# The second attention's values: split float32r products, or float32 products with two experts in one array

## The chip, the cores and the metric

One of the eight cores of a Trainium2 chip runs the whole program; there is one launch. The metric is the device time of that launch in microseconds (us), as a median over runs. Lower is better. TensorE is the matrix engine (PE in the profile, PEld for its weight loads), VectorE is DVE, ScalarE is ACT, GpSimd is POOL, and SyncE (SP) issues most of the DMA transfers.

## What is computed

Three layers follow each other: a linear attention, a feed-forward layer with a layer norm, and a mixture of four attention experts (here "the second attention"). Only the last is touched. Cut from the reference, with B = 8 batches, S = 576 positions, D = 512, E = 4 experts, head size 64:

```python
for e in range(E):
    q = x @ wq[e]
    k = x @ wk[e]
    v = x @ wv[e]
    scores = scale * (q @ k.transpose(0, 2, 1))
    causal = np.triu(np.ones((S, S), dtype=bool), 1)
    scores = np.where(causal, -1000000000.0, scores)
    scores = scores - scores.max(-1, keepdims=True)
    a = np.exp(scores)
    a /= a.sum(-1, keepdims=True) + 1e-09
    ye = a @ v @ wo[e]
    for kk in range(K):
        mask = topk[:, :, kk] == e
        out += mask[..., None] * w[:, :, kk:kk + 1] * ye
```

The change is in how `a @ v` is formed and in when.

## The kernel before, in words

**Numbers in two halves.** Nearly every product of the kernel keeps float32 accuracy by a split: an operand is written as a float32r value plus a float32r rest (ACT writes the first, DVE subtracts it from the source and writes the second; the helper `split`, L180 and L181), and three or four float32r products are added up in PSUM. All products go through the helper `mm`, so they carry line L174 in the profile and are told apart by their output tile: `psh` and `acc` or `psc` for the feed-forward layer, `psqk` for queries and keys, `psv` for values, `pssc` for scores, `pst` for transposes, `py` for attention times values, `pso` for the output projection.

**Where products are float32.** A few early products take float32 operands as they are: `pkv` in the first attention (two heads, each 64 columns of the array, one into PSUM partitions 0 to 63, the other into 64 to 127; 112 or 128 rows, 66 moving columns, called one head after the other for five chunks) and `po<-qT,kvw` (128 columns, 288 moving columns). A float32 product shows as two matmul records.

**The last part of the program** (from about 820 us) goes batch by batch. While the attention of one batch (`back`) runs, the feed-forward layer of the next (`mlp2`) and its projections (`qk_proj`, `v_proj`) run beside it: `weave` deals the pieces of the two lists alternately, and the framework's scheduler then sets the order of the instructions on each engine. For the last batch (`order[-1]`) little is left to deal between.

**A unit** is one row block (128 queries; the fifth block has 64 and takes both experts in one unit, `PairUnit`) of one pair of experts r (r = 0, 1; within it j = 0, 1 are the two experts). It makes scores (`pssc`, then one DVE instruction that adds the mask and finds the bound, L1369), the exponentials (ACT, L1377), the scale by sum and gate (POOL, L1389), and in `turn` transposes the weights on PE (`pst`, L1401 and L1450). `put` copies them out of PSUM as two float32r tiles: ACT writes `aTh` (L1420), then DVE writes the rest `aTl` (L1421), which needs `aTh`.

**values.** Rows are taken in groups (`GROUPS`: blocks 0 and 1, then 2 to 4; in the last batch's r = 1 `LASTG`: 0, then 3 and 4, then 1 and 2). Before, all groups of r = 0 come first and then those of r = 1. When the units of a group are done, `values` forms for each expert j the sum over key blocks kb. The tile `vv` holds for each expert 128 columns: 64 of v's float32r value and 64 of its rest. The stationary operand is these 128 columns, the moving one is `aTh`, then `aTl`: two products for a key block (the last key block has 64 keys, and its rows carry both halves in one product). PSUM `py` then has the two parts in its two halves; ACT copies the lower half out (`ytmp`, L1472), DVE adds the two (`yf`, L1473), and with both experts done `split` writes `yh` and `yl`, which `proj` multiplies with wo.

```python
th, tl = aT[j]
...
parts = (th,) if kb == NQ - 1 else (th, tl)
for t in parts:
    mm(py[:, c0:gn], vt, t[:, offs[kb]:offs[kb] + n], kb == 0 and t is th,
       kb == grp[-1] and t is parts[-1])
tmp = atp.tile([D, GW], F32, tag="ytmp", name="ytmp")
nc.scalar.activation(tmp[:, :gn], py[D:2 * D, :gn], AF.Copy)
nc.vector.tensor_tensor(yf[j * D:(j + 1) * D, :gn], py[:D, :gn], tmp[:, :gn], op=ALU.add)
```

For the group of blocks 0 and 1 the moving columns are 256 and 128 for the two key blocks; for blocks 2 to 4 they are 320, 320, 320, 192 and 64.

Of the kernel before, what the change touches and what calls it, by code (L numbers as in the profile page):

```python
# [18 lines left out]
P = 128  # L19
# [110 lines left out]
def tile_kernel(ctx: ExitStack, tc: tile.TileContext, q, k, v, g_ln, w1, w2, w_gate, wq, wk, wv, wo, out):  # L130
# [1135 lines left out]
    def v_proj(x2s, res):  # L1266
        def one(c):
            if c == 0:
                res["v"] = qkp.tile([P, NQ, E, 2, D], F32R, tag="vv", name="vv")
                res["lg"] = qkp.tile([P, NQ, E], F32, tag="lg", name="lg", bufs=2)  # L1270
                nc.gpsimd.memset(res["lg"], 0.0)
            vv, lg, wvg = res["v"], res["lg"], moe["vg"]
            n = min(P, S - c * P)
            ps = psm("psv")
            h, o = divmod(c * P, T)
            if o + n <= T:
                x = x2s[h][:, :, :, o:o + n]
            else:
                x = res["xj"]
            for cc in range(NDC):  # L1280
                mm(ps[:n, :VG], x[:, 0, cc, :], wvg[:, 0, cc, :], cc == 0, False)
                mm(ps[:n, :VG], x[:, 0, cc, :], wvg[:, 1, cc, :], False, False)
                mm(ps[:n, :VG], x[:, 1, cc, :], wvg[:, 0, cc, :], False, cc == NDC - 1)
            pv = ps[:n, :E * D].rearrange("p (e d) -> p e d", e=E)

            for t in [vv[i:i + n, c] for i in range(0, P, n)]:
                nc.scalar.activation(t[:, :, 0, :], pv, AF.Copy)
                nc.vector.tensor_tensor(t[:, :, 1, :], pv, raw(t[:, :, 0, :]), op=ALU.subtract)
            nc.vector.tensor_copy(lg[:n, c, :], ps[:n, E * D:VG])  # L1289
            for g0, g1 in GCUTS:  # L1290
                if c == g1 - 1:
                    gates(g0, g1)
# [44 lines left out]
            o += gn - max(0, kb * P - g0)  # L1337
        return g0, gn, offs, o

    GW, AW = (max(layout(g)[i] for g in GROUPS + LASTG) for i in (1, 3))  # L1340

    class Unit:

# [8 lines left out]
        def scores(self, j):  # L1352
            r, i, m, w = self.r, self.i, self.m, self.w
            if j == 0:
                self.st = atp.tile([P, 2, 4], F32, tag="st", name="st", bufs=4)
            sm = self.sm[j] = atp.tile([P, S], F32, tag="sm", name="sm", bufs=4)
            mo = NM - i * P
            q = self.res[r, "q"][:, j, i * P:i * P + m]
            self.part(sm, m, 0, w, [(j, q)], mask[:m, mo:mo + w], j, 0)
            self.last = 0  # L1360
# [31 lines left out]
        def turn(self, j):  # L1392

            i, m, sm = self.i, self.m, self.sm[j]
            g0, _, offs, _ = layout(self.grp)
            if i == self.grp[0]:
                self.aT[j] = tuple(atp.tile([P, AW], F32R, tag=nm, name=nm, bufs=2) for nm in ("aTh", "aTl"))
            pt = ps_t.tile([P, 512], F32, tag="t", name="pst")
            for kb in range(i + 1):
                kw = min(P, S - kb * P)  # L1400
                nc.tensor.transpose(pt[:kw, kb * m:kb * m + m], sm[:m, kb * P:kb * P + kw], ident[:m, :m])  # L1401
            dst = [offs[kb] + i * P - max(g0, kb * P) for kb in range(i + 1)]
            self.put(j, pt[:, :(i + 1) * m].rearrange("p (n m) -> p n m", m=m), P, dst, m)

        def put(self, j, src, kw, dsts, m):

            kb = 0
            while kb < len(dsts):

                n = 1  # L1410
                while kb + n < len(dsts) and dsts[kb + n] - dsts[kb + n - 1] == dsts[kb + 1] - dsts[kb]:
                    n += 1
                step = dsts[kb + 1] - dsts[kb] if n > 1 else m
                th, tl = (t[:, dsts[kb]:dsts[kb] + m] for t in self.aT[j])
                oh, ol = (bass.AP(tensor=o.tensor, offset=o.offset, ap=[list(o.ap[0]), [step, n], [1, m]])
                          for o in (th[:kw], tl[:kw] if kw == P else th[kw:]))
                from_ = src[:, kb:kb + n]
                if n == 1:
                    oh, ol, from_ = oh[:, 0], ol[:, 0], src[:, kb]
                nc.scalar.activation(oh, from_, AF.Copy)  # L1420
                nc.vector.tensor_tensor(ol, from_, raw(oh), op=ALU.subtract)  # L1421
                kb += n

    class PairUnit(Unit):
# [6 lines left out]
        def scores(self, j):  # L1431
            if j == 0:
                self.st = atp.tile([P, 2, 4], F32, tag="st", name="st", bufs=4)
                self.sm[0] = atp.tile([P, S], F32, tag="sm", name="sm", bufs=4)
            c0 = j * T
            qs = [(e, q_pads[self.r][:, e, :]) for e in range(2)]
            self.part(self.sm[0], P, c0, c0 + T, qs, tail_mask if j else mask[:, :T], 0, j)
            self.last = 1
# [4 lines left out]
        def turn(self, j):  # L1443
            i, sm = self.i, self.sm[0]
            g0, _, offs, _ = layout(self.grp)
            pt = ps_t.tile([P, 512], F32, tag="t", name="pst")
            blocks = range(i) if j == 0 else (i,)
            for n, kb in enumerate(blocks):
                kw = min(P, S - kb * P)
                nc.tensor.transpose(pt[:kw, n * P:(n + 1) * P], sm[:, kb * P:kb * P + kw], ident)  # L1450
            dsts = [offs[kb] + i * P - max(g0, kb * P) for kb in blocks]
            for e in range(2):
                src = pt[:kw, :len(dsts) * P].rearrange("p (n e m) -> p e n m", e=2, m=ML)[:, e]
                self.put(e, src, kw, dsts, ML)

    def values(res, r, grp, aT, yh, yl, ends_):
        g0, gn, offs, _ = layout(grp)
        yf = atp.tile([P, GW], F32, tag="yf", name="yf", bufs=2)

        def one(j):  # L1460
            th, tl = aT[j]
            py = psy("py")
            for kb in range(grp[-1] + 1):
                c0 = max(0, kb * P - g0)
                n = gn - c0
                vt = res["v"][:, kb, 2 * r + j].rearrange("p t d -> p (t d)")
                parts = (th,) if kb == NQ - 1 else (th, tl)
                for t in parts:
                    mm(py[:, c0:gn], vt, t[:, offs[kb]:offs[kb] + n], kb == 0 and t is th,
                       kb == grp[-1] and t is parts[-1])  # L1470
            tmp = atp.tile([D, GW], F32, tag="ytmp", name="ytmp")
            nc.scalar.activation(tmp[:, :gn], py[D:2 * D, :gn], AF.Copy)  # L1472
            nc.vector.tensor_tensor(yf[j * D:(j + 1) * D, :gn], py[:D, :gn], tmp[:, :gn], op=ALU.add)  # L1473
            if j == 1:
                n = min(gn, S - ML - g0)
                split(yf[:, :n], yh[:, r, g0:g0 + n], yl[:, r, g0:g0 + n])
                if n < gn:
                    split(yf[:, n:gn], ends_[:, 0, r], ends_[:, 1, r])

        return [lambda j=j: one(j) for j in range(2)]  # L1480

    def proj(ys, outs):

# [15 lines left out]
    def back(b, res):  # L1499
# [16 lines left out]
        def project(c):  # L1516
# [5 lines left out]
                                     [out[b_, S - ML:, :] for b_ in bs])]  # L1522
            return []

        us, last = [], {}
        for r in range(NR):
            for grp in (LASTG if b == order[-1] and r == NR - 1 else GROUPS):
                aT = {}
                us += [(Unit if i < NQ - 1 else PairUnit)(res, r, grp, i, aT) for i in grp]
                last[len(us) - 1] = (r, grp, aT)  # L1530
        out_, cut = [], []
        for s in range(len(us) + 2):
            if s - 2 in last:
                r, grp, aT = last[s - 2]
                box = []

                def val(j, r=r, grp=grp, aT=aT, box=box):
                    if not box:
                        box.extend(values(res, r, grp, aT, yh, yl, mine))
                    box[j]()  # L1540

                out_ += [lambda j=j, val=val: val(j) for j in range(2)]
            if s - 3 in last and last[s - 3][0] == NR - 1:
                out_ += [p for c in last[s - 3][1] for p in project(c)]
            if s < len(us):
                if us[s].r == NR - 1:
                    cut.append(len(out_))
                out_ += [lambda u=us[s], j=j: u.scores(j) for j in range(2)]
                out_.append(us[s].exps)
            if 0 <= s - 1 < len(us):  # L1550
                out_.append(lambda u=us[s - 1]: u.turn(0))
            if s < len(us):
                out_.append(us[s].scales)
            if 0 <= s - 1 < len(us):
                out_.append(lambda u=us[s - 1]: u.turn(1))
# [60 lines left out]
```

## Time and profile before

| what | us |
| --- | --- |
| median of 3 runs (lowest, highest) | 1355.36 (1354.23, 1356.77) |
| the profiled execution | 1356.32 |
| its span, first to last instruction | 1354.6 |
| PE busy, of the span | 1297.1 (96%) |
| DVE busy | 889.6 (66%) |
| ACT busy | 687.5 (51%) |
| POOL busy | 342.4 (25%) |

The profile is that of one execution; 1.7 us of it lie outside the span. An engine's busy time counts each instant once. A matmul record lasts from its start until its last column has left the array, so records of a stream overlap: a stream's pace is read from how long a row of many records takes, and not from the mean length of one.

### The profile page before, as it was taken

The page shows a single profiled execution, that of the slowest core. Times are in us where ns is not written, and L with a number is a line of the kernel's source. Part 1 is how long each engine was busy: PE and PEld are TensorE (multiplying, and loading weights), DVE is VectorE, ACT ScalarE, POOL GpSimd, SP SyncE. Part 2 cuts the span into 40 slices and gives each one's busy share as a digit, 9 for nine tenths or more (in the row PEclk, how much of TensorE's full clock was granted, in tenths as well). Part 3 has the DMA queues.
Part 4 walks back from the last instruction along what each step waited for, and adds up shares of the span by engine and source line. Part 5 has one row for each costly group of instructions (what it writes and reads, how often), then busy time and mean ns, then how long its engine had stood idle before and what let it go on. Part 6 is the DMA issues. An engine that isn't in the chain of part 4 may idle for free.

```text
span 1354.6 us, 26863 instructions
## 1 busy us (share of the span) xinstructions
PE 1297.1 (96%) x9932; PEld 1255.8 (93%) x9932; DVE 889.6 (66%) x2602; ACT 687.5 (51%) x1802; POOL 342.4 (25%) x445
## 2 busy tenths in 40 slices
PE   5678999999999999999999999999999999999997
PEld 3578999999999999999999999999999999999995
DVE  7999564654645656456472238777768677776785
ACT  7667443434343434344442135656556656565666
POOL 5756413122131221212240002111211111121211
PEclk9898999999999999999999999999999999999999
DMA  8655232331322324215112023323232332423021
GB/s 228 200 174 150 80 96 72 112 93 50 110 75 94 85 72 114 75 53 156 64 34 47 1 83 121 107 83 106 85 94 90 90 98 62 118 84 86 23 67 56
DMA packets 136772, 124.84 MB, mean 92 GB/s; under 512 B 84160, under 2 KB 124096, under 8 KB 133056
## 3 DMA queue, kind: packets, MB, share of 16 engines
q1 hardware_dynamic: 126176, 97.16, 25.6%
q10 hardware_dynamic: 10464, 25.95, 5.3%
q8 instruction: 79, 1.29, 0.4%
q14 instruction: 53, 0.43, 0.1%
HBM read 74.07 MB, written 35.39 MB: 81 GB/s over the span
## 4 chain that ended last, share of the span: by engine, by line
PE 70%; DVE 4%; DMA 2%; ACT 1%; issue 1%; SPq 0%; POOL 0%; ACTq 0%; DVEq 0%
PE psh L174 21%; PE acc L174 14%; PE psqk L174 7%; PE psc L174 7%; PE pssc L174 4%; PE py L174 4%; PE psv L174 4%; PE pso L174 3%; PE pst L1401 2%; PE po L174 1%; DMA q<-in_q_dram 1%; PE pkv L174 1%; PE pst L1450 1%; DMA k<-in_k_dram 0%; PE pq L510 0%
## 5 line engine op out<-in xcount | busy, mean ns | idle before, releaser
L174 PE MATMUL psh<-xhl,w 128*128 128x288 f32 x3072 | 470.4, 299 | 5.2 <-DVE w L270 2.2
L174 PEld LDWEIGHTS psh<-xhl,w 128*128 128x128 f32 x3072 | 429.7, 190 | 8.6 <-DVE w L270 2.5
L174 PE MATMUL acc<-hh,w 128*128 128x288 f32 x2400 | 371.4, 299 | 10.0 <-DVE hh L714 8.9
L174 PEld LDWEIGHTS acc<-hh,w 128*128 128x128 f32 x2400 | 335.6, 189 | 14.4 <-DVE hh L714 10.9
L714 DVE SCALAR_TENSOR_TENSOR hh<-psh,hh 128x288 fp32r<-128x288 f32 x200 | 90.5, 453 | 159.5 <-ACT hh L711 158.2
L711 ACT ACTIVATE hh<-psh 128x288 fp32r<-128x288 f32 x200 | 81.6, 408 | 170.0 <-PE psh L174 165.2
L1389 POOL TENSOR_SCALAR sm<-sm,st,lg 128x128 f32<-128x128 f32 (+3 forms) x128 | 80.3, 637 | 273.6 <-DVE st L1386 99.1
L174 PE MATMUL psqk<-x,wqk 128*128 128x288 f32 x768 | 112.6, 298 | 0.5 <-DVE lg L1289 0.3
L174 PEld LDWEIGHTS psqk<-x,wqk 128*128 128x128 f32 x768 | 104.7, 188 | 1.8 <-PE pst L1401 0.8
L174 PE MATMUL psc<-hb,w 128*128 128x288 f32 x672 | 100.5, 299 | 0.0
L1377 ACT ACTIVATE sm<-sm,st 128x128 f32<-128x128 f32 (+2 forms) x144 | 83.7, 583 | 17.9 <-DVE st L1369 16.7
L174 PEld LDWEIGHTS psc<-hb,w 128*128 128x128 f32 x672 | 92.4, 189 | 0.3
L1420 ACT ACTIVATE aTh<-pst 128x128 fp32r<-128x128 f32 (+5 forms) x254 | 79.2, 334 | 24.7 <-PE pst L1401 12.2
L1369 DVE CUSTOM_DVE_ANT_0 sm<-pssc,mask 128x128 f32<-128x128 f32 (+2 forms) x144 | 67.7, 482 | 32.2 <-PE pst L1401 19.9
L1421 DVE TENSOR_TENSOR aTl<-pst,aTh 128x384 fp32r<-128x384 f32 (+4 forms) x222 | 82.0, 382 | 9.8 <-ACT aTh L1420 7.1
L476 POOL TENSOR_TENSOR qe<-q,sm 128x320 f32<-128x320 f32 x64 | 47.5, 763 | 87.5 <-PE pkv L515 78.2
L611 POOL TENSOR_TENSOR sq<-sq 128x288 f32<-128x288 f32 x45 | 37.3, 828 | 109.4 <-ACT sq L639 107.4
L174 PE MATMUL py<-aTh,vv 128*128 128x320 f32 (+4 forms) x228 | 58.4, 275 | 1.6 <-DVE yf L1473 0.9
L425 POOL TENSOR_TENSOR q<-q,sm 128x640 f32<-128x640 f32 x28 | 35.9, 1283 | 91.2 <-DVE sm L422 86.2
L174 PE MATMUL pssc<-k,q 128*128 128x128 f32 (+3 forms) x256 | 58.0, 326 | 0.5 <-DVE st L1369 0.5
L263 POOL TENSOR_TENSOR w_t<-w_t,wraw 128x512 int32<-128x512 int32 x32 | 45.2, 1414 | 51.6 <-DVE w_t L259 13.3
L174 PE MATMUL psv<-wvg,x 128*128 128x260 f32 (+1 forms) x384 | 54.3, 285 | 0.0
(174 smaller groups left out, 2115.8 us busy)
## 6 DMA issues: line engine op xcount, KB each, us to landing
wraw<-in_moe_w_ch_dram SPq DMA_DIRECT2D x32, 512.0 KB, 3.9
xn_d<-xhl ACTq DMA_DIRECT2D x14, 1152.0 KB, 5.0
xhl<-xn_d SPq DMA_DIRECT2D x14, 1152.0 KB, 5.1
xp_d<-xT ACTq DMA_DIRECT2D x16, 576.0 KB, 3.6
k<-k SPq DMA_DIRECT2D x32, 288.0 KB, 3.5
k<-in_k_dram SPq DMA_DIRECT2D x32, 256.0 KB, 2.9
q<-in_q_dram SPq DMA_DIRECT2D x32, 256.0 KB, 3.6
out_dram<-ot SPq DMA_DIRECT2D x32, 256.0 KB, 2.0
```

What stands on the lines that cost most here:

```text
L174: nc.tensor.matmul(o, lhsT, rhs, start=start, stop=stop)
L263: nc.gpsimd.tensor_tensor(box[0], box[0], low, op=ALU.add)
L425: nc.gpsimd.tensor_tensor(self.q3, self.q3, self.sm[:, 0, :, None].to_broadcast([P, 2 * NCH, D]), op=ALU.subtract)
L476: nc.gpsimd.tensor_tensor(self.qe[:, :, j, :], self.qt[:, j], self.sm[:, 2, j * NCH:(j + 1) * NCH, None].to_broadcast([P, NCH, D]), op=ALU ...
L611: nc.gpsimd.tensor_tensor(self.t, self.t, self.sq[:, c], op=ALU.add)
L711: nc.scalar.activation(self.hh[:, 0], self.ps, AF.Relu)
L714: nc.vector.scalar_tensor_tensor(self.hh[:, 1], self.ps, 0.0, raw(self.hh[:, 0]), op0=ALU.max, op1=ALU.subtract)
L1369: nc.vector.tensor_tensor_reduce(out=sm[:m, c0:c1], in0=o_, in1=msk, scale=1.0, scalar=3e38 if n == 0 else st[:m, j, 0:1], op0=ALU.add, op ...
L1377: nc.scalar.activation(sm[:m, :w], sm[:m, :w], AF.Exp, bias=st[:m, j, last:last + 1], scale=-1.0, accum_out=st[:m, j, 2:3])
L1389: nc.gpsimd.tensor_scalar(sm[:m, :w], sm[:m, :w], st[:m, j, 3:4], self.gate()[:, j:j + 1], op0=ALU.mult, op1=ALU.mult)
L1420: nc.scalar.activation(oh, from_, AF.Copy)
L1421: nc.vector.tensor_tensor(ol, from_, raw(oh), op=ALU.subtract)
```

## The change

v is kept as one float32 tile (`vv`, 64 columns for an expert; the rows that the fifth key block lacks are set to zero by POOL). `put` writes one float32 tile `aT`: for expert 0 ACT copies, for expert 1 DVE does, with no subtraction. `values` has two pieces: `sums` calls one float32 product for each key block and expert, 64 columns wide, expert 0 into PSUM partitions 0 to 63 and expert 1 into 64 to 127 of the same `py`; `parts` splits `py` directly into `yh` and `yl`. Transposes always fill 128 rows, so score tiles are 640 columns wide and POOL sets the last 64 of a pair unit to zero. In all batches but the last the units go group by group: blocks 0 and 1 of r = 0, then of r = 1, then both pairs' values; then blocks 2 to 4 in the same way.

```diff
@@ v_proj @@
-                res["v"] = qkp.tile([P, NQ, E, 2, D], F32R, tag="vv", name="vv")
+                res["v"] = qkp.tile([P, NQ, E, D], F32, tag="vv", name="vv")
+                nc.gpsimd.memset(res["v"][ML:, NQ - 1], 0.0)
...
-            for t in [vv[i:i + n, c] for i in range(0, P, n)]:
-                nc.scalar.activation(t[:, :, 0, :], pv, AF.Copy)
-                nc.vector.tensor_tensor(t[:, :, 1, :], pv, raw(t[:, :, 0, :]), op=ALU.subtract)
+            nc.scalar.activation(vv[:n, c].rearrange("p e d -> p (e d)"), ps[:n, :E * D], AF.Copy)
@@ turn @@
-                self.aT[j] = tuple(atp.tile([P, AW], F32R, tag=nm, name=nm, bufs=2) for nm in ("aTh", "aTl"))
+                self.aT[j] = atp.tile([P, AW], F32, tag="aT", name="aT", bufs=4)
@@ put @@
-                nc.scalar.activation(oh, from_, AF.Copy)
-                nc.vector.tensor_tensor(ol, from_, raw(oh), op=ALU.subtract)
+                if j == 0:
+                    nc.scalar.activation(o, from_, AF.Copy)
+                else:
+                    nc.vector.tensor_copy(o, from_)
@@ PairUnit.scores @@
-                self.sm[0] = atp.tile([P, S], F32, tag="sm", name="sm", bufs=4)
+                self.sm[0] = atp.tile([P, NQ * P], F32, tag="sm", name="sm", bufs=4)
+                nc.gpsimd.memset(self.sm[0][:, S:], 0.0)
@@ values @@
-            for kb in range(grp[-1] + 1):
-                c0 = max(0, kb * P - g0)
-                n = gn - c0
-                vt = res["v"][:, kb, 2 * r + j].rearrange("p t d -> p (t d)")
-                parts = (th,) if kb == NQ - 1 else (th, tl)
-                for t in parts:
-                    mm(py[:, c0:gn], vt, t[:, offs[kb]:offs[kb] + n], kb == 0 and t is th,
-                       kb == grp[-1] and t is parts[-1])
-            tmp = atp.tile([D, GW], F32, tag="ytmp", name="ytmp")
-            nc.scalar.activation(tmp[:, :gn], py[D:2 * D, :gn], AF.Copy)
-            nc.vector.tensor_tensor(yf[j * D:(j + 1) * D, :gn], py[:D, :gn], tmp[:, :gn], op=ALU.add)
+        def sums():
+            py = psy("py")
+            box.append(py)
+            for kb in range(grp[-1] + 1):
+                c0 = max(0, kb * P - g0)
+                n = gn - c0
+                for j in range(2):
+                    mm(py[j * D:(j + 1) * D, c0:gn], res["v"][:, kb, 2 * r + j], aT[j][:, offs[kb]:offs[kb] + n],
+                       kb == 0, kb == grp[-1])
+        def parts():
+            py = box[0]
+            n = min(gn, S - ML - g0)
+            split(py[:, :n], yh[:, r, g0:g0 + n], yl[:, r, g0:g0 + n])
+            if n < gn:
+                split(py[:, n:gn], ends_[:, 0, r], ends_[:, 1, r])
@@ back @@
-        for r in range(NR):
-            for grp in (LASTG if b == order[-1] and r == NR - 1 else GROUPS):
+        if b == order[-1]:
+            turns_ = [(r, grp) for r in range(NR) for grp in (LASTG if r == NR - 1 else GROUPS)]
+        else:
+            turns_ = [(r, grp) for grp in GROUPS for r in range(NR)]
...
+                out_ += [lambda i=i, n=n, val=val: val(i, n) for n in range(2) for i in range(len(boxes))]
```

Up to the first score of the first batch the order of instructions on TensorE is that of before. From there the scheduler's order is another one. On PE, the second group of a batch's first pair of experts before (first batch of the last part; `pst` are transposes, `psh` is the next batch's feed-forward layer; x12 counts equal instructions in a row):

```order
L1450 MATMUL pst<-ident,sm 64x128
L174 MATMUL py<-aTh,vv 128x320
L174 MATMUL psh_9857<-xhl_9527,w_14_8096 128x288 x12
L174 MATMUL py<-aTl,vv 128x320
L174 MATMUL py<-aTh,vv 128x320
L174 MATMUL py<-aTl,vv 128x320
L174 MATMUL py<-aTh,vv 128x320
L174 MATMUL py<-aTl,vv 128x320
L174 MATMUL py<-aTh,vv 128x192
L174 MATMUL py<-aTl,vv 128x192
```

The two experts' products stood one expert after the other, with other products between them. On PE in the change, the same batch's second group, first for r = 0 and then for r = 1 (`py` 64 wide is one expert's float32 product; experts 0 and 1 alternate, beginning with 0):

```order
L174 MATMUL py<-aT,vv 64x320 x6
L174 MATMUL py<-aT,vv 64x192 x2
L174 MATMUL py<-aT,vv 64x64 x2
L174 MATMUL pssc<-k,q 128x128
L174 MATMUL psqk<-x_9881,wqk 128x288 x24
```

and six rows further on:

```order
L174 MATMUL py<-aT,vv 64x320
L174 MATMUL psv<-wvg,x_9646 128x260 x12
L174 MATMUL py<-aT,vv 64x320 x4
L174 MATMUL psqk<-x_9881,wqk 128x288 x12
L174 MATMUL py<-aT,vv 64x320
L174 MATMUL py<-aT,vv 64x192 x2
L174 MATMUL py<-aT,vv 64x64 x2
```

The first group stands in one run of ten products; the second is cut into three runs by products of another tile, and the cuts part expert 0's product of a key block from expert 1's. Over the whole program the 33 groups stand in 61 such runs (51 with 196 products before the last batch's attention, 10 with 32 products in it).

On DVE, the end of the program before (`yf` adds a product's halves, `aTl` is the rest of the weights, `yhl` and `ye` the rest of the result):

```order
L1473 TENSOR_TENSOR yf<-py,ytmp 64x192
L1421 TENSOR_TENSOR aTl<-pst,aTh 128x2x128
L1473 TENSOR_TENSOR yf<-py,ytmp 64x192
L1421 TENSOR_TENSOR aTl<-pst,aTh 128x2x128
L181 TENSOR_TENSOR yhl<-yf,yhl 128x128
L181 TENSOR_TENSOR ye<-yf,ye 128x64
L1421 TENSOR_TENSOR aTl<-pst,aTh 128x2x128 x2
L1421 TENSOR_TENSOR aTl<-pst,aTh 128x128 x2
L1473 TENSOR_TENSOR yf<-py,ytmp 64x256 x2
L181 TENSOR_TENSOR yhl<-yf,yhl 128x256
```

and on DVE in the change:

```order
L1418 COPY aT<-pst 128x2x128
L181 TENSOR_TENSOR yhl<-py,yhl 128x128
L181 TENSOR_TENSOR ye<-py,ye 128x64
L1418 COPY aT<-pst 128x2x128
L1418 COPY aT<-pst 128x128
L181 TENSOR_TENSOR yhl<-py,yhl 128x256
```

The additions `yf` are gone, and one expert's copies remain of the two experts' subtractions.

## Rows read from the trace of the kernel before

**Rows 1.** The page: busy tenths in 40 slices of the span; PEclk, granted clock.

```profile
PE   5678999999999999999999999999999999999997
...
PEclk9898999999999999999999999999999999999999
```

**Rows 2.** Windows view of all instructions (its first line names the columns).

```profile
core 0: us, PE busy (x) PEld busy (x) DVE busy (x) ACT busy (x) POOL busy (x), PEclk, DMA share, GB/s
...
820.00:1305.00 485.00, 484.80 (x3593) 472.66 (x3592) 357.84 (x1414) 294.91 (x881) 89.88 (x158) 1.00 0.30 89
1305.00:1355.00 50.00, 40.17 (x253) 33.42 (x251) 35.06 (x153) 31.78 (x96) 11.69 (x20) 1.00 0.16 50
```

**Rows 3.** The chain that ended last, 820 to 1305 us: shares; one long piece.

```profile
by line: PE psc L174 18.5%; PE psh L174 18.1%; PE psqk L174 17.4%; PE pssc L174 10.3%; PE psv L174 10.0%; PE py L174 9.1%; PE pso L174 8.3%; PE pst L1401 6.4%; PE pst L1450 1.6%; DVE vv L1288 0.2%; DVE st L1385 0.0%; issue 0.0%; DVE lg L128
...
932.51 4.77 PE psqk L174 x36
```

**Rows 4.** Waits of PE, 820 to 1305 us: total us, times, longest.

```profile
PE psh L174 <- DVE lg L1289: 0.2, 1, 0.2
```

**Rows 5.** Timeline about a run of `pkv`, and elsewhere: start, us it spans, xcount.

```profile
192.40 0.27 PE L515 MATMUL pkv<-ident,qe 128*128 128x128 f32 x1
192.60 0.80 PE L174 MATMUL pkv<-v,ke 112*64 112x66 f32 x20
193.34 1.85 PE L174 MATMUL psh<-xhl,w 128*128 128x288 f32 x12
...
702.22 1.76 PE L174 MATMUL psh<-xhl,w 128*128 128x288 f32 x12
```

**Rows 6.** Timeline inside such a run; tile `pkv`: ns least/median/most.

```profile
652.14 0.40 PE L174 MATMUL pkv<-v,ke 112*64 112x66 f32 x8
...
L174 PE MATMUL pkv<-v,ke x640: 219/222/374, 13.1 to 652.5; 112*64 112x66 f32 x128, 128*64 128x66 f32 x32
```

**Rows 7.** Timeline of a float32 product of 288 columns; tile `kvw`, ns.

```profile
79.54 0.65 PE L174 MATMUL po<-qT,kvw 128*128 128x288 f32 x2
...
L174 PE MATMUL po<-qT,kvw x32: 403/406/849, 19.8 to 148.5; 128*128 128x288 f32 x32
```

**Rows 8.** Windows view of tile `py` alone (PE, PEld, DVE, ACT).

```profile
820.00:1305.00 485.00, 62.60 (x364) 55.14 (x364) 25.17 (x56) 22.84 (x56) 1.00 0.30 89
1305.00:1355.00 50.00, 9.43 (x60) 8.23 (x60) 3.88 (x10) 3.59 (x10) 1.00 0.16 50
```

**Rows 9.** Groups by shape from 820 us: busy us, mean ns, idle before.

```profile
L1421 DVE TENSOR_TENSOR aTl<-pst,aTh 128x384 fp32r<-128x384 f32 x60 | 33.0, 551 | 2.0 <-ACT aTh L1420 1.5
L1473 DVE TENSOR_TENSOR yf<-py,ytmp 64x320 f32<-64x320 f32 x30 | 14.5, 483 | 16.5 <-ACT ytmp L1472 16.2
L1288 DVE TENSOR_TENSOR vv<-psv,vv 128x256 fp32r<-128x256 f32 x28 | 11.7, 421 | 3.0 <-ACT vv L1287 2.6
...
L1420 ACT ACTIVATE aTh<-pst 128x384 fp32r<-128x384 f32 x60 | 28.8, 488 | 6.5 <-PE pst L1401 5.8
...
L1271 POOL MEMSET lg<- 128x20 f32 x6 | 0.7, 114 | 0.4
```

**Rows 10.** The chain that ended last, 1305 us to the end: shares by line.

```profile
by line: PE pso L174 12.3%; PE py L174 11.0%; DVE sm L1369 8.8%; DVE aTl L1421 7.1%; ACT sm L1377 6.2%; issue 4.8%; DVE k L1244 3.7%; DVE q L1244 3.7%; DVE yf L1473 3.7%; ACT aTh L1420 3.0%; ACT ytmp L1472 2.9%; DVE vv L1288 2.4%; PE pssc L
```

## Prediction: what the changed kernel will take

> **What bounds the kernel now.** I read the slices of the page first: TensorE (PE) is busy in nine tenths or more of nearly every slice, at the full granted clock but for the first few [rows 1]. The change touches only the second attention, which begins at about 820 us, so the next view is that of the windows. From 820 to 1305 us PE is busy 484.8 of 485.0 us at clock 1.00 (2.4 GHz), DVE 357.8 and ACT 294.9 [rows 2]; there PE waited 0.2 us in all [rows 4], and nearly all of the chain that ended last is PE, with `py` 9.1% of it [rows 3]. In this stretch (the body) what is added to PE is added to the time, and what is taken from DVE or ACT gives nothing. From 1305 us to the end (the tail: the last batch's attention, with little feed-forward work beside it) PE is busy only 40.2 of 50 us [rows 2], and DVE and ACT stand on the chain by turns with PE [rows 10]. There a shorter chain of copies does give time. So the change is costed twice, once for each stretch. The order of instructions is that of before up to the second attention, so the first 820 us are taken as unchanged.
>
> **What a product costs on PE now.** `py` has 9.1% of 485 us, 44.1 us, of the body's chain [rows 3] for 364 products [rows 8], 0.121 us each. In the tail it has 11.0% of 50 us, 5.5 us [rows 10], for 60 products [rows 8].
>
> **What a float32 product costs.** A float32 product of 288 columns is two records: both span 0.65 us, one lasts 0.406, so the second starts 0.244 us after the first [rows 7]. The product takes 0.488 us, 1.69 ns a column; the float32r products take 4.77 / 36 = 0.1325 us each for 288 columns [rows 3], 0.46 ns a column. One expert's key block before needed two float32r products, both experts four, 1.84 ns a column by this pace. Two float32 products one after the other would be 3.39, two side by side 1.69. All hangs on whether they run side by side, and on what it costs to get in and out.
>
> **Side by side, at a price.** `pkv` has this very form: two float32 products of 64 columns each, into the two halves of one PSUM tile, in turn. The run at 192.60 us holds ten products of 66 columns (20 records). The transpose before it ends at 192.40 + 0.27 = 192.67, and the twelve products after it end at 193.34 + 1.85 = 195.19 [rows 5]. Of these 2.52 us the twelve take 12 x 0.1325 = 1.59 at their usual pace, so the run costs 0.93 us. One after the other, its ten products would take 10 x 66 x 1.69 ns = 1.12 us: they do run side by side. Inside a run, eight records span 0.40 us and one lasts 0.222 [rows 6], so four pairs start within 0.18 us, one each 0.059 us. Ten pairs make 0.59 us, and 0.93 - 0.59 = 0.34 us is what it costs to enter the array's halved form and to leave it again, whatever the length of the run. I take 0.34 for each run, with 0.30 and 0.38 as ends (0.38 if the pairs go at 1.69 ns a column, 0.56 us in all; 0.30 as much below).
>
> Here a page of the Trainium skill says otherwise: "TensorE: Matmul & The Clock Gate", section "Measured speedup vs the span model", gives a packed set the span of one matmul and about 4 ns for each further tile, with no price for entering. By that the 61 runs would cost nothing beyond their columns; the run of `pkv` costs 0.34 us more, so the trace does not agree. It is the second rival below.
>
> **The body, on PE.** The change has 196 float32 products here in 51 runs. Seven batches with two pairs of experts have 14 groups of 256 + 128 = 384 columns and 14 of 3 x 320 + 192 + 64 = 1216, together 22,400 columns; as whole pairs at 1.69 ns they take 37.9 us. But the order cuts 22 pairs, so that one expert's product ends a run and the other's begins the next: 11 of 320 columns, 8 of 256, one of 192, two of 64, 5,888 columns that are paid twice, 9.9 us; in a few runs the lone product has the other expert's next one beside it, and I take 9. The switches are 51 x 0.34 = 17.3 us. Sum 64.2 us against 44.1: **20 us more**.
>
> **The body, elsewhere.** Gone are `ytmp`, `yf`, the rests of v and the subtractions `aTl`, and the copies of `put` fall to one for each expert, ACT's for one and DVE's for the other (0.551 and 0.488 us for 384 columns today [rows 9]). With PE never waiting this is worth nothing. POOL gets 24 small memsets; a like one takes 0.114 us [rows 9] and POOL is busy 89.9 of 485 us [rows 2], so 24 x 0.2 = 5 us of it disappear there. One memset a batch waits until the batch before has read `vv`, with POOL's later scaling queued behind it, as ACT's writing of `vv` did before. SP's queue has the same transfers in a slightly other order; its loads come many microseconds ahead, which I cost at nothing. The held banks are the new wait: both pairs' `py` are kept from `sums` to `parts`, so that `proj` and some projections, which take the same two banks, must wait for two ACT copies and DVE subtractions. Ends for it: 0, since the scheduler put other products between, and half a microsecond at each cut (third rival). I take 0.
>
> **The tail.** There are 3,200 columns (384 + 1216 + 128 + 832 + 640), 5.4 us, five cut pairs with 704 columns, 1.2 us, and ten runs, 3.4 us: 10.0 against 5.5, 4.5 us more. Off the chain of [rows 10] go `ytmp` and `yf` (2.9% + 3.7% of 50 us, 3.3 us), the rests of v (2.4%, 1.2 us) and half of `aTl`, since DVE copies for one expert of two (half of 7.1%, 1.8 us): 6.3 us. Net **2 us less**. The ends are 6.3 less, if PE's idle 9.8 us swallow all of its extra work, and 4.5 more, if what is late next (the bounds `sm` on DVE, 8.8% [rows 10]) keeps the chain where it was.
>
> **Sum.** 20 - 2 = 18 us on the profiled execution of 1356.3 us (span 1354.6 and 1.7 around it) gives 1374.3. The median of the runs shown is 1.0 lower, so I predict **1373 us**, 1.3% slower. With the ends of the switch (2.4 us either way), of the cuts and of the tail this case spans 1366 to 1383.
>
> **The rivals.**
> 1. *Likeliest, chance 0.63*: as summed, 1373.
> 2. *Faster: the switches cost nothing here* (chance 0.06). The 0.34 us of `pkv` could be a wait for its operands, which that run has and these might not. Then the body is 37.9 + 9 - 44.1 = 3 us more, the tail 6.6 - 5.5 - 6.3 = 5 less, and if the shorter chain works off 3 more of the 9.8 idle us there, 5 less in all: 1350. It decides below 0.08 us a run, where 61 runs cost those 5 us. Against it: the twelve products *behind* the run span 1.85 us, and twelve elsewhere 1.76 [rows 5]; a wait for the run's operands would not slow those behind it. The skill's page "TensorEngine Tiling (Array Packing)", section "Key Properties", also says that a change of the tiling mode drains the engine; the 0.34 us agree.
> 3. *New waits at the cuts* (chance 0.16). A cut stands where the scheduler did not hold the second expert's copy ready, and PE is in order. If PE stood for one copy, 0.5 us, at each of the 27 cut pairs, 14 us come on top: 1387.
> 4. *The pairs do not run side by side at 320 columns* (chance 0.06): `pkv` shows it at 66 columns only. Then 22,400 columns are paid twice, 38 - 9 = 29 us more in the body and 4 in the tail: 1406.
> 5. *Less of everything* (chance 0.09): runs cost 0.25 us, the tail gives its whole 6.3 us. 20 - 5 - 6 = 9, less 1 for the median: 1364 or under, towards no change.
>
> **How the numbers follow.** A measurement of this kernel tells about 0.2% (2.7 us) from no change. Slower by more are the cases 1, 3 and 4 (0.85) and the upper part of 5 (0.03): 0.88. Within 0.2% falls the rest of 5, 0.06; faster is case 2, 0.06. The range for 8 in 10 runs from 1360 (into case 5) to 1388 (case 3), which leaves out case 2, case 4 and the edges.
>
> **What would show it.** Right: the PE chain from 820 us longer by about 20 us with `py` near 64 us; in a timeline, a row of twelve products behind a `py` run 0.1 us longer than elsewhere; `py` records with 64 columns of the array in pairs; hardly any PE waits before the tail. Wrong: a `py` run of ten products (1,216 columns a side) that lasts over 3 us means no overlap; PE waits on `aT` or on `py` banks of several microseconds mean case 3; an unchanged pace behind the runs means case 2.

## Result and profile after

The changed kernel takes 1365.94 us (median of 4 runs, 1364.62 to 1366.96) against 1355.66 us (4 runs beside it): ratio 1.0076, 95% interval [1.0058, 1.0093]. It is **10.3 us slower**; 18 us were forecast, and the range from 1360 to 1388 us holds the result. The profiled execution took 1364.62 us with a span of 1362.5.

To compare stages the two traces are cut where their work is the same: at the end of the last `acc` product (799.5 us before, 796.7 after) and at the end of the last `psv` product (1308.5 and 1319.7). Between these marks lies the second attention with feed-forward work beside it (the body), and behind the second mark the last batch's attention (the tail). The windows of before, cut this way:

```profile
core 0: us, PE busy (x) PEld busy (x) DVE busy (x) ACT busy (x) POOL busy (x), PEclk, DMA share, GB/s
799.50:1308.50 509.00, 508.79 (x3780) 496.39 (x3779) 377.61 (x1503) 308.13 (x919) 91.35 (x162) 1.00 0.31 89
1308.50:1354.60 46.10, 36.68 (x224) 30.19 (x224) 31.81 (x132) 30.49 (x92) 11.69 (x20) 1.00 0.17 54
```

and those of after, which answer to [rows 2]:

```profile
796.70:1319.70 523.00, 523.00 (x3794) 479.55 (x3793) 314.93 (x1292) 256.76 (x742) 94.54 (x186) 1.00 0.30 87
1319.70:1362.50 42.80, 38.22 (x245) 29.72 (x243) 23.75 (x103) 23.34 (x68) 11.00 (x20) 1.00 0.18 58
```

PE is busy throughout the body as it was, for 14.0 us longer, at the same granted clock of 1.00. DVE and ACT lose 62.7 and 51.4 us of work there, and none of it shows in the time. The tail is 3.3 us shorter, with more PE work in it: PE's idle time falls from 46.1 - 36.7 = 9.4 us to 4.6. In each, some 4 us of it lie behind PE's last product (4.7 and 3.8), where nothing is left to fill them. (The 2.8 us by which the first part ended earlier are in the same instructions; over the profiles of this study that mark lies between 796.2 and 800.4 us.)

The chain that ended last, body and tail of after, by line; these answer to [rows 3, 10]:

```profile
by line: PE psqk L174 18.5%; PE psc L174 17.2%; PE psh L174 17.1%; PE psv L174 11.2%; PE py L174 10.3%; PE pssc L174 10.1%; PE pso L174 7.9%; PE pst L1397 6.1%; PE pst L1447 1.5%; PE acc L174 0.0%
by line: PE py L174 18.8%; PE pso L174 17.7%; PE psqk L174 14.9%; PE pst L1397 11.1%; PE pssc L174 10.5%; issue 4.4%; ACT ot L1486 3.7%; DVE sm L1366 3.3%; POOL sm L1386 1.9%; DVE aT L1418 1.9%; PE pst L1447 1.7%; ACT sm L1374 1.1%; ACT aT 
```

The body is all PE. In the tail the DVE and ACT shares that stood in [rows 10] (`sm` 8.8%, `aTl` 7.1%, ACT's `sm` 6.2%, `yf`, `ytmp`) have shrunk or gone. The waits of PE from the first mark to the end (total us, times, longest) are two, both in the tail:

```profile
PE py L174 <- ACT aT L1416: 0.4, 1, 0.4
PE pst L1447 <- POOL sm L1386: 0.2, 1, 0.2
```

**What a run costs.** Pieces of the same chain in order of time (start, us, what):

```profile
1301.13 0.68 PE py L174 x2
1301.81 1.79 PE psqk L174 x12
...
1310.09 0.68 PE py L174 x2
1310.77 0.37 PE pssc L174 x2
1311.14 2.20 PE py L174 x16
1313.33 3.08 PE psv L174 x24
...
1316.88 2.87 PE psv L174 x24
1319.75 1.60 PE psqk L174 x12
```

A group of five key blocks has ten products. The run at 1301.13 is a single product of 320 columns, cut off from its group. The runs at 1310.09 and 1311.14 are another group, cut in two: again a single product of 320 columns runs first; the other nine (18 records, 16 of which stand on the chain) follow as four pairs and one alone, 1216 columns to be paid. The single product should take 320 x 1.69 ns + 0.34 = 0.88 us, the long run 2.06 + 0.34 = 2.40. On the chain they take 0.68 (both times) and 2.20, and the rows behind them carry the rest: twelve `psqk` take 1.79 us where twelve elsewhere take 1.60, and 24 `psv` 3.08 where 24 elsewhere take 2.87. So leaving costs 0.2 us, and it stands in the *next* line's account, since a piece of the chain goes from the end of the instruction ahead to its own; entering costs 0.14 and stands in the run's own. The chain's `py` of 10.3% of 523 us, 53.9 us, with 0.2 for each of 51 runs makes 64.1 us for the body; 64.2 were forecast.

Summed record by record over the trace (from the end of the instruction ahead of a run to the end of the one behind it, less that one's usual pace) the body's `py` takes 63.3 us after and 46.3 before, the tail's 10.0 and 12.1; the 12.1 hold waits for copies. I call this sum the PE time of `py` below.

Off PE, the copies that are left cost what [rows 9] showed for ACT and DVE (groups by shape: busy us, mean ns, idle before):

```profile
L1418 DVE COPY aT<-pst 128x384 f32<-128x384 f32 x30 | 16.7, 556 | 3.6 <-PE pst L1397 3.2
L1416 ACT ACTIVATE aT<-pst 128x384 f32<-128x384 f32 x30 | 14.7, 488 | 11.5 <-PE pst L1397 11.3
```

POOL does wait for `vv` to be read, as foreseen, and nobody on the chain waits for POOL because of it (the waits of POOL):

```profile
POOL vv L1270 <- PE py L174: 30.3, 5, 10.1
```

### The profile page after: what moved, and what is told of

Its sections match the earlier page's. It is cut to its first block, busy times and chain, and to the rows that moved or that the text cites. A ratio compares the mean times of both kernels' runs of the same rounds, so it can differ in the third digit from the quotient of the medians.

```text
span 1362.5 us, 26484 instructions
## 1 busy us (share of the span) xinstructions
PE 1317.8 (97%) x9964; PEld 1242.6 (91%) x9964; DVE 817.6 (60%) x2361; ACT 629.1 (46%) x1601; POOL 345.8 (25%) x469
## 4 chain that ended last, share of the span: by engine, by line
PE 72%; DMA 2%; DVE 2%; ACT 1%; issue 1%; SPq 1%; POOL 0%; ACTq 0%; DVEq 0%
PE psh L174 21%; PE acc L174 14%; PE psqk L174 8%; PE psc L174 7%; PE py L174 5%; PE psv L174 4%; PE pssc L174 4%; PE pso L174 4%; PE pst L1397 3%; PE po L174 1%; DMA wraw<-in_moe_w_ch_dram 1%; DMA q<-in_q_dram 1%; PE pkv L174 1%; PE pst L1447 1%; DMA k<-in_k_dram 0%
## 5 line engine op out<-in xcount | busy, mean ns | idle before, releaser
L1386 POOL TENSOR_SCALAR sm<-sm,st,lg 128x384 f32<-128x384 f32 (+3 forms) x128 | 79.2, 628 | 215.3 <-DVE st L1383 86.6
L174 PE MATMUL psqk<-x,wqk 128*128 128x288 f32 x768 | 115.7, 298 | 0.0
L1374 ACT ACTIVATE sm<-sm,st 128x256 f32<-128x256 f32 (+4 forms) x144 | 84.2, 585 | 45.2 <-DVE st L1366 42.9
L1366 DVE CUSTOM_DVE_ANT_0 sm<-pssc,mask 128x256 f32<-128x256 f32 (+4 forms) x144 | 68.8, 484 | 38.9 <-PE pssc L174 29.6
L174 PE MATMUL py<-aT,vv 128*64 128x320 f32 (+3 forms) x456 | 66.2, 364 | 0.4 <-ACT aT L1416 0.4
L174 PE MATMUL pssc<-k,q 128*128 128x128 f32 (+3 forms) x256 | 60.8, 332 | 0.0
L263 POOL TENSOR_TENSOR w_t<-w_t,wraw 128x512 int32<-128x512 int32 x32 | 45.5, 1423 | 49.7 <-DVE w_t L259 12.5
L174 PEld LDWEIGHTS py<-aT,vv 128*64 128x64 f32 x456 | 34.4, 136 | 24.0 <-issue 6.2
L1418 DVE COPY aT<-pst 128x128 f32<-128x128 f32 (+3 forms) x127 | 42.2, 362 | 16.7 <-PE pst L1397 14.4
L174 PE MATMUL psv<-wvg,x 128*128 128x260 f32 (+1 forms) x384 | 51.3, 284 | 0.0
```

What stands on the lines that cost most here:

```text
L174: nc.tensor.matmul(o, lhsT, rhs, start=start, stop=stop)
L263: nc.gpsimd.tensor_tensor(box[0], box[0], low, op=ALU.add)
L1366: nc.vector.tensor_tensor_reduce(out=sm[:m, c0:c1], in0=o_, in1=msk, scale=1.0, scalar=3e38 if n == 0 else st[:m, j, 0:1], op0=ALU.add, op ...
L1374: nc.scalar.activation(sm[:m, :w], sm[:m, :w], AF.Exp, bias=st[:m, j, last:last + 1], scale=-1.0, accum_out=st[:m, j, 2:3])
L1386: nc.gpsimd.tensor_scalar(sm[:m, :w], sm[:m, :w], st[:m, j, 3:4], self.gate()[:, j:j + 1], op0=ALU.mult, op1=ALU.mult)
L1418: nc.vector.tensor_copy(o, from_)
```

## The experiments

My theory after the result: the body pays for switches and cut pairs as forecast, and something else makes the sum smaller. The first rival: PE waits at new places. The runs of `py` come first (e1 to e4 and e8), then the tail (e5 to e7 and e9 to e11). All start from the changed kernel or the kernel before, as each says.

### e1: each group in one run

The products of a group are kept together by priority, and the first waits for the copies of both experts; no pair is cut.

```diff
-            for kb in range(grp[-1] + 1):
...
+            with tc.high_priority():
+                for kb in range(grp[-1] + 1):
...
+                        if kb == 0 and j == 0:
+                            for i in copied[id(aT)].values():
+                                tc.add_manual_dep(traced()[-1], i.name, SYNC, reason="both experts at once")
```

> The changed kernel, with each group's products in one uncut run on PE: the first product waits for both experts' copies, the run has high priority. 33 runs in place of 61, no cut pair in place of 27. Theory 'switches and cuts' (a run costs about 0.35 us to enter and leave, a cut pair pays its columns twice): 28 x 0.35 = 9.8 us and about 9.7 us for the cut pairs come off the change's 1365.9, so 1346 us, 0.7% below the kernel before. Rival 'new waits' (the loss comes from PE waiting on copies and held PSUM banks): waiting for both copies makes it no better, 1363 us or more.

Measured: 1353.42 us (10 runs), 0.9985 of before [0.9975, 0.9995], 7 us above the theory's time. The PE time of `py` is 54.4 us: all 25,600 columns (body and tail) in whole pairs at 1.69 ns are 43.3 us, and 33 runs of 0.34 are 11.2, together 54.5. So the price is as in the theory, but of the 19.0 us that `py` is shorter than in the changed kernel, 12.5 arrive. Some 4 us of the rest are idle time of PE that the changed kernel doesn't have: 2.9 us in the body, where it had none, and 5.8 against 4.6 us in the tail. I have not traced the remaining 2.5. Windows (body, tail), and waits of PE in the body:

```profile
799.30:1310.20 510.90, 508.04 (x3792) 475.43 (x3791) 313.27 (x1288) 255.97 (x739) 95.17 (x185) 1.00 0.31 89
1310.20:1352.10 41.90, 36.13 (x248) 29.53 (x246) 23.72 (x106) 24.23 (x72) 11.08 (x20) 1.00 0.19 59
...
PE pssc L176 <- DVE q L1246: 1.0, 2, 0.5
PE psqk L176 <- DVE k L1246: 0.9, 2, 0.6
PE pssc L176 <- DMA k<-k: 0.8, 1, 0.8
```

### e2: both pairs of experts in one run

e1, and in all batches but the last the runs of the two pairs of experts are joined; the first product waits for the copies of all four experts.

```diff
+                def both(val=val, k=len(boxes)):
+                    n0 = len(traced())
+                    for i in range(k):
+                        val(i, 0)
+                    in_order(traced()[n0:])
```

> As the run with whole runs, and the two pairs of experts of a group share one run in all batches but the last: 21 runs. 'Switches and cuts': another 12 x 0.35 = 4.2 us less, 1342 us. Rival 'new waits': the first product now waits for four copies, so PE idles more and it is slower than whole runs by several us.

Measured: 1354.54 us (10 runs), 0.9998 [0.9987, 1.0008]. The 12 runs fewer take 3.85 us off the PE time of `py` (50.5; 43.3 + 21 x 0.34 = 50.4): **0.32 us for each**. The time does not follow: it is 1.1 us above e1, where the theory had 4 us less. PE now waits longer, for the transfer `k<-k` and for DVE's splitting of `q` and `k`:

```profile
800.00:1313.00 513.00, 505.20 (x3790) 476.51 (x3789) 309.70 (x1287) 254.40 (x738) 96.73 (x185) 1.00 0.30 88
...
PE pssc L176 <- DMA k<-k: 3.4, 2, 1.8
PE psqk L176 <- DVE q L1246: 2.3, 1, 2.3
PE psqk L176 <- DVE k L1246: 1.9, 1, 1.9
```

My reading, which no run tries: the more the products are gathered, the less is left to lay between the projections and the scores that need them. The changed kernel itself has none of these waits.

### e3: one expert's products, then the other's

e1, with all products of expert 0 in a group ahead of those of expert 1, and held in that order (`in_order`).

```diff
-                for kb in range(grp[-1] + 1):
+                for j in range(2):
+                    for kb in range(grp[-1] + 1):
...
-                    for j in range(2):
```

> As whole runs, with the same 33 runs, but within a run all products of expert 0 come before those of expert 1, so that no two neighbours use different halves of the array. If neighbours in the two halves run side by side, 25,600 columns are paid twice: 25,600 x 1.69 ns = 43 us more than whole runs, about 1389 us. If the halves overlap whatever the order, or not at all, the time is that of whole runs.

Measured: 1380.77 us (2 runs), 1.019 of before [1.017, 1.021], 27.3 us above e1, which shows that side by side is real; but it is less than forecast. Runs of eight records (two key blocks) take as long as in e1, and only the runs of twenty are longer. Timelines of e1, then of e3 (start, us spanned, xcount; the row of a run of eight and of one of twenty):

```profile
826.89 0.87 PE L176 MATMUL py<-aT,vv 128*64 128x256 f32 x8
...
858.68 2.27 PE L176 MATMUL py<-aT,vv 128*64 128x320 f32 x20
```

```profile
828.01 0.88 PE L176 MATMUL py<-aT,vv 128*64 128x256 f32 x8
...
859.80 3.94 PE L176 MATMUL py<-aT,vv 128*64 128x320 f32 x20
```

### e4 and e8: the order of the units

e4 is e1, e8 the changed kernel, each with the units in the order of the kernel before.

```diff
-        if b == order[-1]:
-            turns_ = [(r, grp) for r in range(NR) for grp in (LASTG if r == NR - 1 else GROUPS)]
-        else:
-            turns_ = [(r, grp) for grp in GROUPS for r in range(NR)]
+        turns_ = [(r, grp) for r in range(NR) for grp in (LASTG if b == order[-1] and r == NR - 1 else GROUPS)]
...
-            if b == order[-1] or r == NR - 1:
+            if True:
```

> As whole runs, but with the units in the order of the kernel before (all groups of one pair of experts, then those of the other). 'Switches and cuts': the same 33 runs, so within 2 us of whole runs. Rival 'the order pays or costs by itself' (output projections come earlier, two banks are held at once): a difference of 4 us or more, in either direction.

> The changed kernel with its units in the order of the kernel before (all groups of one pair of experts, then of the other), its runs cut where the scheduler cuts them. Theory (the cost lies in switches and cut pairs, the order of the units is worth little): as many runs and cuts within a few, 1365 us plus or minus 3. Rival (the order group by group gathers the products and is worth the switches it saves): 1369 us or more.

Measured: e4 1351.53 us (10 runs), 0.9969 [0.9958, 0.9979], 1.9 us under e1; e8 1369.80 us (4 runs), 1.0109 [1.0095, 1.0123], 3.9 us above the changed kernel. In e8 there are 65 runs instead of 61 and the PE time of `py` is 2.5 us more: where the scheduler is left to cut, the order group by group does save switches, and the rival of e8 was right. Where nothing is cut, the order is worth less than 2 us, as the theory of e4 had it, and the other way: e4 has as many runs as e1, and PE idles 1.2 us in the body instead of 2.9.

### e5: the change without its tail

The first seven batches as changed, the last batch's attention as before (the change's code is taken where a flag is set; what the fifth key block lacks is set to zero in `aT` and not in the scores):

```diff
+            if nb != order[-1]:
+                res["whole"] = True
```

> The change in the first seven batches (cut runs, units group by group), while the last batch's second attention is computed as in the kernel before. Theory (the body costs what was forecast, and the tail gives more than the 2 us forecast, some 7, because products, copies and sums of the last batch wait for one another): 1355.7 + 17.5 = 1373 us, 7 us slower than the changed kernel. Rival (the body costs less than forecast, about 12 us, and the tail gives the forecast 2): 1368 us.

Measured: 1369.76 us (4 runs), 1.0108 [1.0094, 1.0122]. It fell between theory and rival. The body costs **14.3 us**, not 20; the change's tail gives 1369.76 - 1365.94 = **3.8 us**, not 2. Its windows:

```profile
797.90:1321.10 523.20, 523.20 (x3796) 479.68 (x3795) 315.40 (x1294) 256.26 (x742) 95.64 (x199) 1.00 0.30 87
1321.10:1367.90 46.80, 38.88 (x240) 32.06 (x238) 32.72 (x132) 31.07 (x94) 11.62 (x20) 0.98 0.17 53
```

The body is that of the changed kernel within 0.2 us. In the tail PE is 2.2 us busier than before (38.9 against 36.7) and the stretch is only 0.7 us longer. The scheduler has pushed 11 `psqk` and 4 `pssc` products from the body across the second mark (12 and 4 in the changed kernel), where they fall into PE's idle time.

### e6 and e11: the tail alone

The kernel before, with float32 products in the last batch alone; in e6 each group in one run as in e1, in e11 cut as in the change.

```diff
+            if nb == order[-1]:
+                res["whole"] = True
```

> The kernel before, with float32 products in the last batch's second attention alone, each group's products there in one uncut run (the padding of the last key block is cleared in aT by POOL). Theory (the tail's chain of copies and sums is what the change shortens): PE has 6 runs and 3,200 columns there, 5.4 + 6 x 0.34 = 7.4 us against 5.5, and the chain loses 7 to 9 us: 1348 to 1350 us, the fastest kernel of the study. Rival (what the tail gains is given back by the longer products, as the sum of the forecast has it for cut runs): 1354 to 1356 us.

> The kernel before with float32 products in the last batch alone, its runs cut where the scheduler cuts them, as in the change. Theory (the change's own tail is worth what the run with the last batch as before showed, 3.8 us, and the cuts in the tail cost the other 3): 1351 to 1352 us. Rival (the cuts in the tail lie beside waits and cost nothing, and what the change's tail lacks is lost to the extra key and query products that the body pushes into it): 1348 to 1349 us.

Measured: e6 1348.41 us (5 runs), 0.9953 [0.9939, 0.9966], **the fastest kernel of the study**, as its theory had it; e11 1351.48 us (8 runs), 0.9969 [0.9958, 0.9980]. e11 gives 4.3 us, as the 3.8 of e5 foretold, and whole runs 3 us more. Tails of e6, then of e11 (all instructions, then tile `py` alone: PE, PEld, DVE, ACT):

```profile
1307.60:1347.00 39.40, 33.64 (x229) 26.64 (x227) 22.06 (x101) 22.30 (x66) 10.21 (x20) 0.99 0.20 63
```

```profile
1305.20:1347.90 42.70, 37.40 (x228) 27.33 (x226) 22.48 (x100) 22.18 (x66) 10.22 (x20) 1.00 0.18 58
...
1305.20:1347.90 42.70, 9.29 (x64) 4.85 (x64) 2.25 (x7) 2.03 (x7) 1.00 0.18 58
```

PE has 3.8 us less to do in e6 and idles about as long (5.8 and 5.3 us): the cuts are paid in the tail too, and the rival of e11 falls.

### e7, e9 and e10: which copies

The kernel before with parts of the last batch's work left out: e7 the low copies, e9 the sums of the two halves, e10 both. The two edits:

```diff
-                nc.vector.tensor_tensor(ol, from_, raw(oh), op=ALU.subtract)
+                if kw < P or not self.res.get("no_low"):
+                    nc.vector.tensor_tensor(ol, from_, raw(oh), op=ALU.subtract)
...
+            if res.get("no_sum"):
+                n = min(gn, S - ML - g0)
+                h = slice(j * D, (j + 1) * D)
+                split(py[:D, :n], yh[h, r, g0:g0 + n], yl[h, r, g0:g0 + n])
...
+                return
```

> The kernel before, but in the last batch the copies of the low parts aTl are left out for the full key blocks and the second product of each block reads the high part again, so PE's work is the same and the low part of the probabilities is left out of the sum; yf and ytmp stay. Theory (copies stand on the chain of the tail): DVE's aTl is 7.1% of 50 us there, 3.5 us, so 1352 us. Rival (the copies run beside other work and the tail's gain comes from yf and ytmp alone, or from elsewhere): 1355.7 us.

> The kernel before, but in the last batch ytmp and yf are left out: each expert's sum is split straight from the upper half of py, and the share of v's low part (the lower half) is left out of the sum; PE's work and the copies aTh and aTl stay. Theory (the sums stand on the tail's chain by themselves): 2.8 + 3.6% of 50 us, 3.2 us, go: 1352 to 1353 us. Rival (the tail has several chains side by side, and one alone gives nothing, as with the copies): 1355 us.

> The kernel before, in the last batch without the low copies and without ytmp and yf (the two leavings-out of the runs before together: the low part of the probabilities and of v); PE's work is as before. Theory (copies and sums stand on chains side by side, and both must go): 1349 to 1350 us, nearly what the float32 products in the last batch alone give. Rival (that gain comes from the products' own form, fewer and with both experts at once): 1353 us or more.

Measured: e7 1354.74 us (10 runs), 0.9995 [0.9986, 1.0004]; e9 1354.67 us (12 runs), 0.9990 [0.9981, 0.9999]; e10 1352.15 us (8 runs), 0.9970 [0.9959, 0.9981]. The copies alone give nothing that can be told (0.7 us), the sums alone 1.1 us, both together 3.6. The theories of e7 and e9 fell, and the one of e10 held in kind, 2 us short.

For the copies alone, the waits of PE in the tail of before, and then of e7, show why:

```profile
PE pst L1450 <- DVE st L1385: 0.9, 1, 0.9
PE py L174 <- DVE yf L1473: 0.9, 2, 0.7
PE pssc L174 <- DVE st L1369: 0.7, 2, 0.5
PE pst L1450 <- DVE aTl L1421: 0.6, 1, 0.6
```

```profile
PE pst L1451 <- POOL sm L1389: 1.9, 2, 1.4
PE pst L1401 <- POOL sm L1389: 1.0, 1, 1.0
PE pst L1401 <- ACT aTh L1420: 0.6, 1, 0.6
```

With the low copies gone, PE gets to the transposes sooner and waits there for POOL's scaling of `sm`: a chain that lay beside the copies takes over.

e9 and e10 take off less than their names say. Each expert's sum is split by itself there, where before one split takes both. Tile `yhl` in the tail of before, then of e9 (PE, PEld, DVE, ACT):

```profile
1308.50:1354.60 46.10, 7.39 (x24) 4.06 (x24) 2.02 (x5) 1.85 (x5) 1.00 0.17 54
1307.50:1352.60 45.10, 6.40 (x24) 4.28 (x24) 3.62 (x10) 3.31 (x10) 0.98 0.17 55
```

Of the 3.9 us of `yf` on DVE and 3.6 of `ytmp` on ACT, 1.6 and 1.5 come back in this way. The change has no such second split, so what its missing sums are worth is not shown by these runs; they may be worth more.

## Why the prediction was right, and where its sizes were off

The sign, the place and the mechanism were right; the sum of +18 us was 7.7 too large. The result lies at the lower edge of what the likeliest case spanned (1366 to 1383 us), and both stretches came out faster than summed. By the steps:

- **PE bounds the body; what DVE and ACT lose gives nothing.** Right: PE 523.0 of 523.0 us busy, no wait.
- **0.34 us for each run, 1.69 ns a column for a pair, side by side at 320 columns too.** Right. Three kernels with 61, 33 and 21 runs have 73.4, 54.4 and 50.5 us of `py`; the terms give 74.2, 54.5 and 50.4. Rival 2 (no price) and rival 4 (no overlap) are excluded by these, rival 4 also by e3. The Trainium skill's page "TensorE: Matmul & The Clock Gate", section "Measured speedup vs the span model", has only some 4 ns for a further tile. Inside a run of e1 the two of a pair do start 7 ns apart (at 858.68 us), but the switch is 0.32 us in e2, and the measurement decides.
- **20 us more in the body.** Measured 14.3 (e5). `py` after was sized well, 63.3 us for 64.2. What failed is the price of `py` before, "44.1 us, of the body's chain": the chain books what a narrow product delays in the instruction behind it to that instruction, 2.4 us before, all behind products of 64 to 192 columns. By records the price is 46.3, and the excess of `py` 63.3 - 46.3 = 17.0 us. Against it stand 2.0 us less of `psqk` (1.57) and `pssc` (0.46), the 12 and 4 products that went across the mark and fell into the tail's idle time: I had taken the scheduler's other placements as neutral. The last 0.9 us less are a wait of 0.2 that is gone and 0.7 in the five other lines, which have as many products as before; these I have not traced. 17.0 - 2.0 - 0.9 = 14.1, where the windows have 14.0.
- **New waits at the cuts or at the held banks, taken as 0** (rival 3). Right: PE waits 0.6 us in all. The one mechanism that I had not seen is the reverse: PE comes to wait when runs are *not* cut (e1, e2).
- **The tail 2 us less.** Measured 3.8, within its ends. Both of its steps were too large, and their errors partly cancel, so it is in part luck that the miss is small. In "10.0 against 5.5, 4.5 us more" the 10.0 came, but 5.5 is only what lay of `py` on a chain that passes from engine to engine: PE was busy with `py` for 9.43 us before [rows 8], and for 9.29 in e11. All of the tail's PE is 0.7 us busier in e11, and the stretch 3.4 us shorter. The "6.3 us" of copies and sums were added up from shares of the chain. e7 takes off all that `aTl` had, 7.1% and by that 3.5 us, and gives 0.7 that can't be told from nothing. Shares of a chain beside which another lies don't add. How much too large the part of the sums was stays open, since e9 and e10 put splits in.
- **Rival 5** came nearest by its number, but not by its price of 0.25 us a run, which e1 and e2 exclude.

What stays open: why DVE's splits and `k`'s transfer come late in e1 and e2. A kernel with whole runs in which those are moved ahead was not tried.

## What to carry to other kernels

Here products in halves of the array cost what their pairs cost side by side and 0.34 us for each run, short or long: count runs and cut pairs first, then columns. Read a price from the rows *behind* a group too, since a chain books the way out to the neighbour; and where the chain passes from engine to engine, take an engine's work from its busy time and not from its share of the chain. And where PE is the bound, a change that trades PE time for copies belongs only where PE waits: here in the last batch alone it turns +10.3 us into -4.3 with the scheduler's cuts and -7.1 with whole runs.

## What the runs showed of the hardware

In e3 each group's products are queued expert by expert, yet PE overlaps them: it starts a product of the other half ahead of earlier records of the first. In the run of twenty, this begins when only the last four of expert 0's ten records are left. The windows of tile `py` (the run's first 1.60 us, then 0.75), of e3 and then of e1:

```profile
859.75:861.35 1.60, 1.55 (x6) 0.88 (x7) 0.00 (x0) 0.00 (x0) 1.00 0.35 134
861.35:862.10 0.75, 0.75 (x9) 0.47 (x7) 0.00 (x0) 0.00 (x0) 1.00 0.00 0
```

```profile
858.63:860.23 1.60, 1.55 (x12) 0.92 (x14) 0.00 (x0) 0.00 (x0) 1.00 0.35 133
```

The records are told apart by their columns: one of 320 that follows one of 192 can only be expert 1's. Six records start in the time of twelve; then seven start within 0.75 us (two of the nine counted had begun before), the four of expert 0's last blocks beside the first three of expert 1. In a run of eight, where expert 0 has four records, the two experts start 13 ns apart. That four records are the reach is read off these two kinds of run, and was not tried by itself. The Trainium skill's page "TensorE: Matmul & The Clock Gate", section "The mechanism", has matmuls start and end strictly in program order; this trace does not agree where the next product belongs to the other half.
